# A split attention and feed-forward kernel: the weights' float32 words by an integer add on VectorE, their second parts by one subtraction

## The chip, the cores and the metric

The kernel runs on one core of one Trainium2 chip. The core has TensorE (matmuls, written PE), VectorE (DVE), ScalarE (ACT), GpSimd (POOL) and SyncE (SP, which here only issues transfers). The engines run side by side, each takes its own instructions in the order of the program, and they wait for each other by semaphores. The metric is the device time of one execution in microseconds; the time before is the median of three runs.

## The reference

Block-causal attention over 8 batches of 8 heads, then a feed-forward layer with a maximum over three products:

```python
# q, k, v: 8 x 8 x 576 x 64, float32; w1, w2, w3: 512 x 768, w_out: 768 x 512, float64
scores = scale * np.matmul(q, k.transpose(0, 1, 3, 2))
scores = np.where(block_i >= block_j, scores, -1000000000.0)   # blocks of 64
attn = np.exp(scores - np.max(scores, axis=-1, keepdims=True))
attn = attn / (np.sum(attn, axis=-1, keepdims=True) + 1e-09)
x = np.matmul(attn, v)                                         # as 4608 x 512
h = np.maximum(np.maximum(x @ w1, x @ w2), x @ w3)
return (h @ w_out).astype(np.float32)
```

The weights come as float64, two 32-bit words each. The chip has no float64, so the kernel makes of each weight two parts, a first one `h` rounded to fp32r (the format of TensorE's one-pass matmul) and a second one `l` with what the rounding left.

## The kernel before

**Attention** goes by pairs of heads. A pair loads q and k, transposes them (on VectorE by `turn_qk`, L918; for batch 0 on TensorE, L825), forms the scores (qk, L934 and L941), takes row minima on VectorE (L423), exponentials on ScalarE (L607, L961), scales them on GpSimd or ScalarE (L441, L439), transposes them (L630 and L634; for batch 0 on TensorE, L559 and L987) and multiplies with v (pv, L1001). The result is split into `xh` (ScalarE) and `xl` (GpSimd, L254).

**The feed-forward part** goes by chunks of half a batch (256 or 320 rows). `product` (L1119) forms x times w for six column blocks f and three matrices, each as three fp32r matmuls (wh xh, wh xl, wl xh) over four row blocks. The maximum is taken on VectorE (L1134), split again (`hh`, `hl`), and `project` (L1185) multiplies it with w_out, 128 rows of w_out at a time (`wo` 0 to `wo` 5), three matmuls each.

**The weights** come in 24 units of 128 x 512 numbers: units 0 to 17 are the column blocks of w1, w2 and w3, units 18 to 23 the row blocks of w_out. GpSimd issues the load of a unit (`load`, L293). Then come, before the change:

- `size` (ScalarE, L303): the absolute value of the high words, read as float32;
- `clamp`, `shift`, `sign` (VectorE, L309, L316, L322): limits, a shift by three bits and the sign, which give the float32 `a` that has the float64's upper bits;
- `power` (VectorE, L328): the power of two of `a`; `rest` (VectorE, L339): the low word times that power, `c`, in the tile `left`;
- `high` (ScalarE, L249): `h`, that is `a` rounded to fp32r;
- `whole` (TensorE, L346 to L348): a - h + c in PSUM, by three products with the identity (`plus`) and its negative (`less`); the first is fp32, which runs as two instructions, the others fp32r;
- `lower` (ScalarE, L249): the copy out of PSUM, rounded to fp32r, is `l`.

`a` and one more tile of a unit lie in the place of a w_out tile that isn't loaded yet (`wo0` to `wo5`), for the last two units in output buffers (`osb`). So the loads of w_out wait until such a unit is done.

**The order** of all this is made by a planner (`in_order`): every step is a job with a cost on one engine or a choice of engines, a rank, and slots that it takes and gives; whichever engine is free takes the ready job of the lowest rank. The ranks of a weight unit are `DELAY + PACE * u`. A change of one job's cost or engine moves jobs of all engines.

## Time and profile before

| | us |
|---|---|
| median of three runs | 912.27 |
| lowest, highest run | 911.9, 914.06 |
| span of the profiled execution | 912.0 |
| TensorE busy in it | 892.8 |
| VectorE busy in it | 529.3 |
| ScalarE busy in it | 471.7 |
| GpSimd busy in it | 254.8 |

The profile comes from one execution, whose span, from its first to its last instruction, is 912.0 us. Its page cuts the span into 40 equal slices (22.8 us each) and gives for each the busy share of an engine in tenths (9 is 90% or more) and the clock that TensorE was granted:

```profile
PE   6999899999999999999999999999999999999998
DVE  4999888786545756564555746564554756421111
ACT  3887675666544635545543645546553644522111
PEclk9899999999999999999999999999999999999999
```

The first seven slices, up to 160 us, hold the preparation of the weights, the attention of batch 0 and part of batch 1's, and the first chunk. Behind them TensorE is busy nearly all the time; in the last four there is no attention left.

### The profile page before, as it was taken

What the parts mean: (1) busy time and instruction counts of PE and PEld (TensorE: products, weight loads), DVE (VectorE), ACT (ScalarE), POOL (GpSimd) and SP (SyncE); (2) the same over time, 40 slices, a digit from 0 to 9 for tenths busy, and PEclk for the clock granted to TensorE, in tenths of its full rate; (3) what the DMA queues carried; (4) which work ended last, traced back from release to release, by engine and by line L of the source; (5) the groups of instructions that cost most, each with busy time, mean ns of one, the idle gap of its engine ahead of it and who ended that gap; (6) DMA issues with size and microseconds to landing.
All of it is one profiled execution on the core that took longest, in us unless ns stands there. A gap on an engine that the chain in (4) does not pass through costs nothing.

```text
span 912.0 us, 16897 instructions
## 1 busy us (share of the span) xinstructions
PE 892.8 (98%) x5880; PEld 743.1 (81%) x5880; DVE 529.3 (58%) x1545; ACT 471.7 (52%) x1365; POOL 254.8 (28%) x381
## 2 busy tenths in 40 slices
PE   6999899999999999999999999999999999999998
PEld 4577677777888888888888888888888888899997
DVE  4999888786545756564555746564554756421111
ACT  3887675666544635545543645546553644522111
POOL 3553232243221312223221322233131322222100
PEclk9899999999999999999999999999999999999999
DMA  5772645776554544454554543555553533330010
GB/s 163 202 217 50 135 116 116 167 150 144 106 135 110 104 101 90 115 118 115 112 130 97 105 108 89 125 113 121 112 123 87 118 82 83 97 73 24 1 36 23
DMA packets 226132, 98.36 MB, mean 108 GB/s; under 512 B 189696, under 2 KB 218368, under 8 KB 226048
## 3 DMA queue, kind: packets, MB, share of 16 engines
q1 hardware_dynamic: 208192, 82.35, 40.6%
q0 software_dynamic: 3456, 12.58, 4.4%
q10 hardware_dynamic: 14400, 2.36, 1.4%
q8 instruction: 46, 0.75, 0.3%
q14 instruction: 38, 0.31, 0.1%
HBM read 41.94 MB, written 9.44 MB: 56 GB/s over the span
## 4 chain that ended last, share of the span: by engine, by line
PE 90%; DVE 5%; DMA 1%; ACT 1%; issue 1%; ACTq 0%; POOL 0%; DVEq 0%
PE pm L1119 50%; PE pm L1185 16%; PE sb L1001 10%; PE sb L934 8%; PE sb L941 3%; PE pm L346 1%; DMA nat<-in_q_dram 1%; DVE sb L423 1%; DVE left L339 1%; DVE wo L322 1%; PE sb L559 1%; DMA nat<-in_k_dram 0%; DVE kq L251 0%; ACT p L439 0%; PE pm L348 0%
## 5 line engine op out<-in xcount | busy, mean ns | idle before, releaser
L1119 PE MATMUL pm<-xh,w 128*128 128x320 f32 (+1 forms) x2304 | 498.6, 303 | 0.7 <-ACT xh L249 0.5
L1119 PEld LDWEIGHTS pm<-xh,w 128*128 128x128 f32 x2304 | 378.8, 189 | 18.8 <-issue 14.0
L1119 PE MATMUL pm<-xl,w 128*128 128x256 f32 (+1 forms) x1152 | 340.7, 296 | 0.5 <-DMA nat<-in_k_dram 0.5
L1119 PEld LDWEIGHTS pm<-xl,w 128*128 128x128 f32 x1152 | 218.5, 190 | 6.7 <-issue 5.3
L423 DVE CUSTOM_DVE_ANT_0 sb<-sb,mask 128x512 f32<-128x512 f32 (+3 forms) x288 | 143.7, 530 | 133.5 <-PE sb L941 76.1
L607 ACT ACTIVATE p<-sb,nm 128x256 f32<-128x256 f32 (+3 forms) x256 | 133.9, 527 | 80.2 <-DVE nm L423 73.7
L1134 DVE TENSOR_TENSOR m<-pm,m 128x256 f32<-128x256 f32 (+1 forms) x192 | 85.9, 448 | 147.9 <-PE pm L1119 147.1
L441 POOL TENSOR_TENSOR p<-p,rs 128x128 f32<-128x128 f32 (+4 forms) x133 | 97.9, 755 | 253.9 <-DVE rs L751 194.5
L630 DVE STREAM_TRANSPOSE pz<-p 128x512 f32<-128x512 f32 (+1 forms) x280 | 137.7, 527 | 36.0 <-ACT p L439 19.1
L254 POOL TENSOR_TENSOR hl<-m,hh 128x256 fp32r<-128x256 f32 x96 | 71.5, 745 | 248.4 <-ACT hh L249 216.5
L1185 PE MATMUL pm<-wo,hh 128*128 128x512 f32 x384 | 119.2, 392 | 0.0
L439 ACT ACTIVATE p<-p,rs 128x512 f32<-128x512 f32 (+4 forms) x155 | 88.2, 597 | 20.6 <-DVE rs L751 14.1
L249 ACT CAST hh<-m 128x256 fp32r<-128x256 f32 x96 | 38.8, 405 | 110.1 <-DVE m L1134 109.1
L934 PE MATMUL sb<-kq 64*128 64x256 f32 (+3 forms) x512 | 89.1, 466 | 3.2 <-DVE kq L251 3.1
L1001 PE MATMUL sb<-pt,vn 128*64 128x320 f32 (+4 forms) x840 | 90.2, 363 | 0.4 <-DVE pt L251 0.3
L254 POOL TENSOR_TENSOR xl<-x,xh 128x256 fp32r<-128x256 f32 (+1 forms) x64 | 52.7, 829 | 130.9 <-ACT xh L249 130.9
L1001 PEld LDWEIGHTS sb<-pt,vn 128*64 128x64 f32 x840 | 55.1, 137 | 34.5 <-issue 1.7
L1185 PEld LDWEIGHTS pm<-wo,hh 128*128 128x128 f32 x384 | 70.9, 188 | 14.9 <-issue 0.3
L934 PEld LDWEIGHTS sb<-kq 64*128 64x128 f32 x512 | 46.3, 192 | 38.1 <-issue 20.8
L1185 PE MATMUL pm<-wo,hl 128*128 128x512 f32 x192 | 74.9, 390 | 0.0
L249 ACT COPY osb<-pm 128x512 f32<-128x512 f32 x36 | 21.1, 587 | 69.5 <-PE pm L1185 67.4
L249 ACT COPY m<-pm 128x256 f32<-128x256 f32 (+1 forms) x96 | 38.1, 397 | 32.6 <-PE pm L1119 23.9
(82 smaller groups left out, 764.0 us busy)
## 6 DMA issues: line engine op xcount, KB each, us to landing
pt<-pz SPq DMA_DIRECT2D x224, 200.0 KB, 3.9
w<-in_moe_w_dram POOLq DMA_DIRECT2D x18, 512.0 KB, 5.2
vn<-in_v_dram SPq DMA_DIRECT2D x64, 128.0 KB, 2.4
out_dram<-osb SPq DMA_DIRECT2D x32, 256.0 KB, 2.0
nat<-in_k_dram SPq DMA_DIRECT2D x112, 72.0 KB, 2.4
nat<-in_q_dram SPq DMA_DIRECT2D x96, 72.0 KB, 2.5
wo<-in_moe_w_out_dram POOLq DMA_DIRECT2D x6, 512.0 KB, 4.4
nat<-in_q_dram ACTq DMA_DIRECT2D x16, 72.0 KB, 4.3
```

What stands on the lines that cost most here:

```text
L249: nc.scalar.copy(dst, src)
L254: {"DVE": nc.vector, "POOL": nc.gpsimd}[eng].tensor_tensor(out=dst, in0=a, in1=b, op=ALU.subtract)
L423: nc.vector.tensor_tensor_reduce(out=ps, in0=ps, in1=hidden, scale=-SCALE, scalar=first, op0=ALU.add, op1=ALU.min, accum_out=out_)
L439: nc.scalar.mul(p, p, r)
L441: nc.gpsimd.tensor_tensor(out=p, in0=p, in1=r.broadcast_to([P, p.shape[1]]), op=ALU.mult)
L607: nc.scalar.activation(dst, src, AF.Exp, bias=nm[:, c : c + 1], scale=-1.0, accum_out=sm[:, c : c + 1])
L630: nc.vector.transpose(dst, p[:, 0 : n * P])
L934: nc.tensor.matmul(ps, self.q[h.own, P * t : P * (t + 1)], self.k[h.own, 0:w], start=True, stop=True)
L1001: nc.tensor.matmul(o[h.own].rearrange("p (i u) -> p i u", u=n)[:, :, c0 : c0 + z - a], self.vn[:, kt, h.j, :], h.pt[:, :, h.off + a : h.of ...
L1119: nc.tensor.matmul(self.ps, w[i, f][:, c, :], xx, start=(c == 0 and s == 0), stop=(c == NC - 1 and s == 2))
L1134: nc.vector.tensor_tensor(out=m, in0=ps, in1=m, op=ALU.max)
L1185: nc.tensor.matmul(self.po[: self.rows], h, w[f], start=(f == 0 and s == 0), stop=(f == NF - 1 and s == 2))
```

## The change

The float32 word is now made whole before it is split. A new step `tail` takes the low word times 2^-29 as an integer (the bits that `shift` left out, rounded), on ScalarE or VectorE as the planner chooses; `whole` is one integer add of these bits to `a`, on VectorE; `high` rounds the sum to `h` as before; `lower` is one subtraction a - h, on GpSimd or VectorE. `power` and `rest`, the three products with the identity, the copy out of PSUM, the tile `less` and the use of `left` by the weights are gone. The temporary tiles are now given back by `lower`.

```diff
-    less = const.tile([P, P], F32R, name="less")
-    nc.scalar.mul(less, one, -1.0)
...
-            for step, fast in (
-                (self.clamp, True),
-                (self.shift, True),
-                (self.sign, False),
-                (self.power, True),
-                (self.rest, False),
-            ):
+            k = job({"ACT": act(512, False) + 65.0, "DVE": dve(512) + 80.0}, rank, self.tail, after=(j,))
+            for step, fast in ((self.clamp, True), (self.shift, True), (self.sign, False), (self.whole, False)):
                 c = dve(512, fast) + (130.0 if fast else 80.0)
-                e = "DVE"
-                j = job({e: c}, rank, step, after=(j,), take=("left",) if step == self.rest else (), lasts=c + GAP)
-            j = job({"ACT": act(512, False)}, rank, self.high, after=(j,))
-            j = job({"PE": 6 * pe(512)}, rank, self.whole, after=(j,), take=("pm",), give=(*self.temps, "left"))
-            self.done = job({"ACT": act(512)}, rank, self.lower, after=(j,), give=("pm",))
+                j = job({"DVE": c}, rank, step, after=(j, k) if step == self.whole else (j,), lasts=c + GAP)
+            h = job({"ACT": act(512, False)}, rank, self.high, after=(j,))
+            self.done = job({"POOL": pool(512), "DVE": dve(512) + 80.0}, rank, self.lower, after=(h,), give=self.temps)
...
+        def tail(self, eng):
+            b = self.parts()[1].bitcast(I32)
+            if eng == "ACT":
+                nc.scalar.mul(b, self.low_word, 2.0**-29)
+            else:
+                nc.vector.tensor_scalar(out=b, in0=self.low_word, scalar1=2.0**-29, scalar2=None, op0=ALU.mult)
...
         def whole(self, eng):
-            self.ps = psm.tile([P, 512], F32, name="pm")
-            nc.tensor.matmul(self.ps, plus.bitcast(F32), self.a, start=True, stop=False)
-            nc.tensor.matmul(self.ps, less, self.h, start=False, stop=False)
-            nc.tensor.matmul(self.ps, plus, self.c, start=False, stop=True)
+            a = self.a.bitcast(I32)
+            nc.vector.tensor_tensor(out=a, in0=a, in1=self.b.bitcast(I32), op=ALU.add)
...
         def lower(self, eng):
-            copy(eng, self.l, self.ps)
+            minus(eng, self.l, self.a, self.h.bitcast(F32))
```

The planner gives 19 of the 24 `tail` steps to ScalarE and 5 to VectorE, and 14 of the 24 `lower` steps to GpSimd and 10 to VectorE. In the changed kernel line numbers differ: L423 becomes L408, L1119 becomes L1104, L1185 becomes L1170, L1001 becomes L986, L934 becomes L919, L309, L316 and L322 become L312, L319 and L325; the integer add is L333. A number behind a name tells copies of a tile apart.

TensorE, before, at the end of the first stretch: the last unit's products and the first projection that needs `wo` 5 (`wo_1799`).

```order
L934 MATMUL sb<-kq 128x256 x2
L346 MATMUL pm<-osb,plus 128x512
L347 MATMUL pm<-wo_1799,less 128x512
L348 MATMUL pm<-left,plus 128x512
L1001 MATMUL sb<-pt,vn_75 64x320 x6
L1001 MATMUL sb<-pt,vn_75 64x4x48 x2
L1001 MATMUL sb<-pt,vn_75 64x4x16 x2
L1185 MATMUL pm<-wo_1799,hh_1616 128x512 x2
```

Now, ahead of the projection that needs `wo` 5 (`wo_1627`):

```order
L1104 MATMUL pm<-xh_1333,w_656 128x320
L1104 MATMUL pm<-xl_1350,w_656 128x320
L1104 MATMUL pm<-xh_1333,w_656 128x320
L1104 MATMUL pm<-xh_1474,w_656 128x320
L1104 MATMUL pm<-xl_1483,w_656 128x320
L1104 MATMUL pm<-xh_1474,w_656 128x320
L1170 MATMUL pm<-wo_1627,hh_1319 128x512 x2
```

The three products with the identity are gone, the pv group that stood between them and the projection has moved behind it, and products stand there; between the projections that need `wo` 4 and `wo` 5 are 36 of them and one qk group (two L919 of 512, 384 and 128 columns each).

VectorE, before, the steps of the last unit (its tiles are `osb` and `wo_1598`) among the attention's reductions:

```order
L309 TENSOR_SCALAR osb<-osb 128x512
L423 ISA sb,nm<-sb,mask 128x128
L423 ISA nm 128x1
L316 TENSOR_SCALAR osb<-osb 128x512
L423 ISA sb,nm<-sb,mask 128x384
L423 ISA nm 128x1
L322 SCALAR_TENSOR_TENSOR osb<-wo_1598,osb 128x512
L423 ISA sb,nm_1769<-sb,mask 128x512
L423 ISA nm_1769 128x1
L328 TENSOR_SCALAR osb<-osb 128x512
L423 ISA sb,nm_1769<-sb,mask,nm_1769 128x64
L423 ISA nm_1769 128x1
```

Now, from the subtraction of the unit before it (`wo_1530`) to the last integer add:

```order
L252 TENSOR_TENSOR wo_1530<-osb,wo_1530 128x512
L1119 TENSOR_TENSOR m<-pm,m 128x320
L957 SCALAR_TENSOR_TENSOR rs_1487<-sm_1486 128x1
L903 STREAM_TRANSPOSE kq<-nat 128x1152
L312 TENSOR_SCALAR osb<-osb 128x512
L963 RECIPROCAL rs_1487<-rs_1487 128x1
L319 TENSOR_SCALAR osb<-osb 128x512
L732 TENSOR_SCALAR rs<-sm 128x2
L325 SCALAR_TENSOR_TENSOR osb<-wo_1441,osb 128x512
L736 RECIPROCAL rs<-rs 128x2
L333 ISA osb<-osb 128x1024
```

The reductions that stood between the last unit's steps stand elsewhere, and the unit ends with the add, which the order prints with 1024 columns.

GpSimd, now, at the loads of w_out (before, no subtraction of weights stood there):

```order
L252 TENSOR_TENSOR w_1183<-wo_941,w_1183 128x512
L284 DMA wo_1209<-in_moe_w_out_dram 128x1024
L252 TENSOR_TENSOR w_1215<-wo_966,w_1215 128x512
L284 DMA wo_1249<-in_moe_w_out_dram 128x1024
L252 TENSOR_TENSOR wo_1285<-wo_1198,wo_1285 128x512
```

The loads now follow subtractions on the same engine.

More of the change, by code (lines that the diff above doesn't have):

```diff
@@ L295, in load, with parts @@
             self.low_word, self.high_word = lo_hi[:, :, 0].bitcast(U32), lo_hi[:, :, 1]
-        def size(self, eng):
-            if len(self.temps) == 1:
-                w = moe.tile([P, 2, 512], F32, name=self.temps[0], bufs=1)
-                self.a, self.b = w[:, 0], w[:, 1]
-            else:
-                self.a, self.b = (moe.tile([P, 512], F32, name="osb", bufs=slots["osb"]) for _ in range(2))
-            nc.scalar.activation(self.a, self.high_word.bitcast(F32), AF.Abs)
+        def parts(self):
+            if not hasattr(self, "a"):
+                if len(self.temps) == 1:
+                    w = moe.tile([P, 2, 512], F32, name=self.temps[0], bufs=1)
+                    self.a, self.b = w[:, 0], w[:, 1]
+                else:
+                    self.a, self.b = (moe.tile([P, 512], F32, name="osb", bufs=slots["osb"]) for _ in range(2))
+            return self.a, self.b
+        def tail(self, eng):
+            b = self.parts()[1].bitcast(I32)
+            if eng == "ACT":
+                nc.scalar.mul(b, self.low_word, 2.0**-29)
+            else:
+                nc.vector.tensor_scalar(out=b, in0=self.low_word, scalar1=2.0**-29, scalar2=None, op0=ALU.mult)
+        def size(self, eng):
+            nc.scalar.activation(self.parts()[0], self.high_word.bitcast(F32), AF.Abs)
         def clamp(self, eng):
@@ L324, in sign @@
             )
-        def power(self, eng):
-            nc.vector.tensor_scalar(
-                out=self.b.bitcast(I32),
-                in0=self.a.bitcast(I32),
-                scalar1=-(2**23),
-                scalar2=None,
-                op0=ALU.bitwise_and,
-            )
-        def rest(self, eng):
-            parts = moe.tile([P, 2, NF, P], F32R, name="left", bufs=1)
-            self.c = parts[:, 0, 0:4].rearrange("p f q -> p (f q)")
-            nc.vector.scalar_tensor_tensor(
-                out=self.c, in0=self.low_word, scalar=2.0**-52, in1=self.b, op0=ALU.mult, op1=ALU.mult
-            )
         def whole(self, eng):
-            self.ps = psm.tile([P, 512], F32, name="pm")
-            nc.tensor.matmul(self.ps, plus.bitcast(F32), self.a, start=True, stop=False)
-            nc.tensor.matmul(self.ps, less, self.h, start=False, stop=False)
-            nc.tensor.matmul(self.ps, plus, self.c, start=False, stop=True)
+            a = self.a.bitcast(I32)
+            nc.vector.tensor_tensor(out=a, in0=a, in1=self.b.bitcast(I32), op=ALU.add)
         def high(self, eng):
```

## The prediction

> **What bounds the kernel now.** I read the engines' shares first, then the busy times by stretch, then the chain of work that ended last. The first line is the page's list of engines (busy us, share of the span, instructions). The next three are stretches that I chose: start:end, length, busy us and instructions of PE, PEld, DVE, ACT and POOL, granted clock, DMA share and rate.
>
> ```profile
> PE 892.8 (98%) x5880; PEld 743.1 (81%) x5880; DVE 529.3 (58%) x1545; ACT 471.7 (52%) x1365; POOL 254.8 (28%) x381
> 0.00:20.00 20.00, 12.03 (x50) 8.26 (x50) 8.01 (x36) 6.78 (x22) 6.82 (x19) 1.00 0.61 170
> 20.00:148.10 128.10, 121.55 (x702) 87.08 (x702) 114.99 (x293) 95.74 (x255) 48.21 (x61) 0.97 0.57 145
> 153.30:912.00 758.70, 754.08 (x5099) 644.77 (x5097) 401.59 (x1202) 365.62 (x1075) 198.10 (x300) 1.00 0.45 101
> ```
>
> From 153.3 us on TensorE lacks 4.6 us of being always busy, and VectorE is at 53%: that stage is worth what TensorE has to do in it. From 20 to 148.1 us it is different: TensorE is busy 121.6 of 128.1 us, but VectorE 115.0 of them, with 13.1 us idle. Both engines are nearly full there, and all weight products that the change drops lie in this stretch, but for unit 23's just behind it. So the question is which of the two ends it afterwards.
>
> Where the stretch ends is in the timeline and in the chain (start us, length us, what):
>
> ```profile
> 147.39 0.69 DVE L339 SCALAR_TENSOR_TENSOR left<-wo,osb 128x512 fp32r<-128x512 uint32 x1
> 149.58 1.05 PE pm L346 x2
> 150.64 0.23 PE pm L347
> 150.87 0.24 PE pm L348
> 151.10 2.21 PE sb L1001 x20
> 151.59 0.59 ACT L249 CAST wo<-pm 128x512 fp32r<-128x512 f32 x1
> 153.31 5.00 PE pm L1185 x21
> ```
>
> VectorE's last weight step ends at 148.1 us, the products of unit 23 at 151.1, its second part at 152.2; at 153.3 TensorE takes the first projection that needs `wo` 5. I call this the anchor, since it stands in both orders with nearly the same work behind it, and TensorE cannot pass it before all weights are there.
>
> **What goes from TensorE.** One unit, in the timeline:
>
> ```profile
> 72.91 1.02 PE L346 MATMUL pm<-wo,plus 128*128 128x512 f32 x2
> 73.37 0.79 PE L347 MATMUL pm<-w,less 128*128 128x512 f32 x1
> 74.00 0.39 PE L348 MATMUL pm<-left,plus 128*128 128x512 f32 x1
> 74.23 0.98 PE L987 MATMUL sb<-plus,p 128*128 128x128 f32 x5
> ```
>
> From 72.91 to 74.23 is 1.32 us of TensorE for a unit (the listed lengths overlap), 24 units 31.7 us. Were TensorE the only bound, this would be the gain. It isn't: behind it stands VectorE's queue.
>
> **What VectorE has to do up to the anchor.** Groups with line, form, count, then busy us and mean ns of one:
>
> ```profile
> L328 DVE TENSOR_SCALAR wo<-wo 128x512 int32<-128x512 int32 x22 | 10.7, 489 | 0.0
> L328 DVE TENSOR_SCALAR osb<-osb 128x512 int32<-128x512 int32 x2 | 0.8, 400 | 0.0
> L339 DVE SCALAR_TENSOR_TENSOR left<-w,wo 128x512 fp32r<-128x512 uint32 x18 | 13.0, 724 | 1.3 <-PE pm L348 1.3
> L339 DVE SCALAR_TENSOR_TENSOR left<-wo,wo 128x512 fp32r<-128x512 uint32 x4 | 3.4, 852 | 0.1
> L339 DVE SCALAR_TENSOR_TENSOR left<-wo,osb 128x512 fp32r<-128x512 uint32 x2 | 1.3, 664 | 0.0
> L322 DVE SCALAR_TENSOR_TENSOR wo<-w,wo 128x512 int32<-128x512 int32 x18 | 12.9, 723 | 0.1
> L918 DVE STREAM_TRANSPOSE kq<-nat 128x1152 f32<-128x1152 f32 x28 | 38.1, 1361 | 3.4 <-DMA nat<-in_q_dram 3.1 <-PE sb L934 0.2
> ```
>
> Removed are `power` (L328) and `rest` (L339): 10.7 + 0.8 + 13.0 + 3.4 + 1.3 = 29.2 us, and L339's wait of 1.3 us for TensorE. Added are 24 integer adds, which the trace does not show. The nearest row is L322: two sources of 512 words, 0.72 us. The order prints the add as 128x1024, and L918 takes 1361 ns for 1152 columns, 1.21 us for 1024: that is the upper end; the one-source L328, 0.49, is the lower. I take 0.72, because the words are 512: 24 x 0.72 = 17.4 us. Ten of the 24 subtractions stand on VectorE, two sources again: 7.2 us. Five `tail` steps stand there, between L328 and L322, say 0.6: 3.0 us. Added in all 27.6, so the edit itself takes only 1.6 us off VectorE.
>
> What else moved is counted in the two orders, up to the last `rest` before and the last add now: 100 rows of L423 for 114, so 7 reductions with their 7 accumulator reads fewer; no L630 or L634 transposes for 12; 38 copies of L251 for 35.
>
> ```profile
> L423 DVE CUSTOM_DVE_ANT_0 sb<-sb,mask 128x512 f32<-128x512 f32 (+3 forms) x288 | 143.7, 530 | 133.5 <-PE sb L941 76.1 <-PE sb L934 45.9 <-ACT p L607 6.7
> L630 DVE STREAM_TRANSPOSE pz<-p 128x512 f32<-128x512 f32 (+1 forms) x280 | 137.7, 527 | 36.0 <-ACT p L439 19.1 <-POOL p L441 14.7
> L251 DVE COPY pt<-sb 128x256 f32<-128x256 f32 (+3 forms) x12 | 4.7, 400 | 0.1
> ```
>
> 7 x 0.53 + 12 x 0.53 - 3 x 0.40 = 8.8 us moved behind the anchor. VectorE's work from 20 us on becomes 115.0 - 29.2 + 27.6 - 8.8 = 104.6 us, 10.4 less.
>
> **ScalarE and GpSimd.** 24 copies out of PSUM go from ScalarE, 19 `tail` steps come; 14 subtractions come on GpSimd.
>
> ```profile
> L249 ACT CAST w<-pm 128x512 fp32r<-128x512 f32 x18 | 10.5, 585 | 4.8 <-PE pm L348 2.1 <-PE sb L559 1.5 <-PE pm L1119 1.2
> L303 ACT ACTIVATE wo<-w 128x512 f32<-128x512 f32 x18 | 12.4, 699 | 1.4 <-issue 1.1 <-ACT wo L303 0.4
> L441 POOL TENSOR_TENSOR p<-p,rs 128x512 f32<-128x512 f32 x27 | 29.2, 1087 | 4.6 <-PE sb L1001 4.3 <-DVE rs L751 0.4
> 66.05 3.28 POOL L441 TENSOR_TENSOR p<-p,rs 128x384 f32<-128x384 f32 x3 [1.44 <-DVE rs L751]
> 66.53 1.90 DVE L309 TENSOR_SCALAR wo<-wo 128x512 f32<-128x512 f32 x2
> L309 DVE TENSOR_SCALAR wo<-wo x22: 396/426/1366, 19.5 to 122.1; 128x512 f32<-128x512 f32 x22
> L309 DVE TENSOR_SCALAR wo<-wo 128x512 f32<-128x512 f32 x22 | 12.5, 579 | 1.6 <-ACT wo L303 1.6
> ```
>
> ScalarE: 24 x 0.59 = 14.0 off, 19 x 0.70 = 13.3 on, no change. GpSimd: 14 x 1.09 = 15.2 us on, in a stretch where it was busy 48.2 of 128.1 us, 38%. That has a price on VectorE: two clamps (L309) took 1.90 us while GpSimd's tensor operations ran; the line's durations are 396 at least and 579 ns on average, 0.18 lost per instruction. 48 of this kind stay (L309 and L316), 8.8 us lost at 38%; at (48.2 + 15.2) / 119.9 = 53% it would be 3.5 us more.
>
> VectorE's last add then ends at 148.1 - 10.4 - 1.3 + 3.5 = 139.9 us, with the rest of its idle time left as it is: waits for TensorE may shrink, but waits for ScalarE's `tail` and `high` come instead.
>
> **From there to the anchor.** `wo` 5 still needs the cast (0.59, as the copy above), the subtraction on GpSimd (1.09) and three hand-overs, 0.4 us in all by my estimate (the one above, from TensorE to ScalarE, took at most 151.59 - 151.11 = 0.48): 139.9 + 0.59 + 1.09 + 0.4 = 142.0 us. Beside it runs TensorE's own queue: `wo` 4 has its subtraction on VectorE ten rows before the last add: L918 1.36, two at 0.72, clamp and shift at 0.58, one max step and four short ones, an estimated 1.3 together, so 5.3 us. Its projection starts at 139.9 - 5.3 + 0.2 = 134.8; then one qk group, 36 products and the projection itself stand before the anchor.
>
> ```profile
> 117.43 1.93 PE sb L934 x12
> 127.38 1.04 PE sb L941 x4
> 832.65 31.99 PE pm L1119 x222
> 205.60 8.38 PE pm L1185 x36
> ```
>
> 1.93 + 36 x 0.144 + 3 x 0.233 = 7.8 us: 142.6. The later of the two, **142.6**, is the anchor now, 10.7 us earlier.
>
> Behind it TensorE's order has 12 products of 320 columns fewer (-1.7), one pv group more (+2.2, L1001 above), one L941 pair (+1.0) and two of L934's twelve (+0.6, by columns): 2.1 us more. So the span becomes 912.0 - 10.7 + 2.1 = 903.4, and 0.3 lies around it (the median of the runs is 912.27, the profiled span 912.0): **903.7 us**, 0.9% faster. TensorE's 31.7 us go, and some 21 come back as its idle time ahead of the anchor.
>
> **Rivals.**
>
> *TensorE sets the pace throughout*: the whole 31.7 us, 880.6. Against it: VectorE would have to do its 104.6 us between 20 us and about 117. Chance 0.03.
>
> *VectorE closes its gaps.* With TensorE no longer full, the 13.1 us idle and the 3.5 for GpSimd may go; all of it gives 888, half 896. For it: some of the gaps are waits for TensorE. Chance 0.14, 888 to 896.
>
> *The integer add is dear* (the other side). Each 0.1 us on it is 2.4 us on VectorE's queue ahead of the anchor, with nothing to cover it. From 0.72 + 8.6 / 24 = 1.08 us on nothing is gained; at L918's rate, 1.21, the time is 915.5. Against it: the words are 512. Chance 0.10. The Trainium skill, "VectorE: DVE Perf Modes", section "The perf-mode tier table", gives two-source operations two 16-bit elements a cycle but one of fp32; were the 1024 elements run one a cycle, an estimate by that page's formula is (1024 + 151) / 0.96 GHz = 1.22 us, and no run here shows it yet.
>
> *TensorE's clock falls.* Three stretches of 5 us: busy us and instructions of PE, granted clock, DMA share, GB/s.
>
> ```profile
> 20.00:25.00 5.00, 3.04 (x18) 0.94 0.66 148
> 25.00:30.00 5.00, 4.69 (x15) 0.50 0.64 211
> 30.00:35.00 5.00, 5.00 (x29) 0.88 0.86 265
> ```
>
> After 5 us with TensorE 61% busy the clock was 0.50 for 5 us, which costs 2.5 us and 0.9 in the two beside it. Ahead of the anchor TensorE would now be busy 12.0 + 121.6 + 5.2 (148.1 to 153.3, all busy) - 31.7 - 2.1 = 105.0 of 142.6 us, 74%, so this may come back several times. TensorE has some 21 us of slack there, so most is hidden; where a reduction on VectorE waits for qk, one to four such falls could give 905 to 917. Chance 0.12. The Trainium skill, "TensorE: Matmul & The Clock Gate", section "What's actually happening", has the array at half clock after an idle window of about 3.4 us and at full clock after as long a busy one; the half clock at 25 us agrees with it, and by that rule short gaps such as these would cost nothing.
>
> *The last weights arrive late*, since GpSimd issues their loads behind a subtraction that waits for ScalarE: 905 to 914, chance 0.06. That the products stay is excluded by TensorE's order.
>
> **Chances and range.** The forecast itself, 896 to 910, has 0.55. Below 896 lie 0.17; the dear add, the clock and the loads hold 0.28. A measurement tells 0.3%, 2.7 us, from no change: faster 0.52 + 0.17 + 0.05 + 0.04 = 0.78, the same 0.03 + 0.03 + 0.03 + 0.01 = 0.10, slower 0.12. The range, 890 to 914, takes in half-closed gaps and most of the dear add, and leaves out about 0.2.
>
> **What would show it.** Right: no L346 to L348; the integer add at 0.6 to 0.8 us; VectorE still about 88% busy from 20 us to its last add, near 140 us; TensorE some 30 us idle before that and at most 5 after; the projection that needs `wo` 5 near 143 us. Wrong: adds over 1 us, a last add before 132 or after 146 us, clamps well above 0.64 us, or more idle time of TensorE behind the anchor than before, which would mean that the attention work moved behind it costs there.

## The result, and the profile after

| | us |
|---|---|
| median of four runs after | 919.72 (918.77 to 922.85) |
| median of four runs before, beside them | 912.16 (911.9 to 914.06) |
| ratio | 1.0074, 95% interval 1.0049 to 1.0098 |
| span of the profiled execution after | 921.1 |

The change makes the kernel 0.7% slower; forecast were 903.7 us and 0.9% faster. The profiled execution is the run of 922.85 us, 3.1 us above the median, so the sums below are of this one execution.

From the page of the changed kernel, its list of engines and the slices (23.0 us each now) of two of them and of the clock:

```profile
PE 878.3 (95%) x5784; PEld 736.1 (80%) x5784; DVE 539.1 (59%) x1538; ACT 469.5 (51%) x1354; POOL 278.8 (30%) x398
...
PE   6787789999999999999999999999999999999998
...
DVE  4999989876664656464664656464664655421111
...
PEclk9979889999999999999999999999999999999999
```

In the first six slices TensorE has gaps now and a lower clock, and VectorE is as full as before. Three stretches of the same kernel (start:end, length, busy us and instructions of PE, PEld, DVE, ACT and POOL, granted clock, DMA share, GB/s):

```profile
0.00:20.00 20.00, 12.24 (x51) 8.42 (x52) 8.01 (x36) 7.21 (x23) 6.97 (x19) 1.00 0.60 170
20.00:150.37 130.37, 103.58 (x608) 76.82 (x608) 118.41 (x261) 90.25 (x232) 70.11 (x76) 0.88 0.49 129
152.42:921.10 768.68, 760.43 (x5115) 648.77 (x5113) 410.68 (x1238) 371.38 (x1099) 199.65 (x302) 1.00 0.45 102
```

TensorE has lost 14.5 us of busy time in all, but stands idle for 42.8 us (921.1 - 878.3) where it was 19.2. From 20 us to the end of the last integer add VectorE has 118.4 us to do in 130.4; before it had 115.0 in 128.1. So the queue that sets the end of this stretch has not become shorter, although 32 instructions fewer were recorded in it (293 before). TensorE's clock is 0.88 there, and was 0.97. From the timelines of TensorE and VectorE of the changed kernel, the places that the prediction named:

```profile
144.21 0.75 PE L1170 MATMUL pm<-wo,hh 128*128 128x512 f32 x2
149.65 0.69 DVE L333 CUSTOM_DVE_ANT_0 osb<-osb 128x1024 uint16<-128x1024 uint16 x1
152.42 0.77 PE L1170 MATMUL pm<-wo,hh 128*128 128x512 f32 x2
```

These are the projection of `wo` 4, the last add and the projection of `wo` 5, which is the anchor: 152.4 us, where 142.6 had been forecast and 153.2 stood before. Behind it 768.7 us follow; 758.8 stood before and 760.8 were forecast. The miss of 17.7 us in the span is 9.8 us at the anchor and 7.9 behind it.

What fills VectorE shows in its groups between 20 us and its last weight step. First three of the kernel before (the sign, the clamp and the old steps stand in the prediction), then the changed kernel's; count, then busy us and mean ns of one.

```profile
L316 DVE TENSOR_SCALAR wo<-wo 128x512 int32<-128x512 int32 x22 | 11.8, 547 | 0.1
L972 DVE SCALAR_TENSOR_TENSOR rs<-sm 128x1 f32<-128x1 f32 x5 | 1.3, 255 | 0.0
L747 DVE TENSOR_SCALAR rs<-sm 128x4 f32<-128x4 f32 x6 | 1.0, 170 | 0.2 <-ACT p L607 0.2
```

```profile
L333 DVE CUSTOM_DVE_ANT_0 wo<-wo 128x1024 uint16<-128x1024 uint16 x22 | 17.7, 806 | 0.0
L325 DVE SCALAR_TENSOR_TENSOR wo<-w,wo 128x512 int32<-128x512 int32 x18 | 14.6, 809 | 0.1
L325 DVE SCALAR_TENSOR_TENSOR wo<-wo,wo 128x512 int32<-128x512 int32 x4 | 3.9, 967 | 0.0
L319 DVE TENSOR_SCALAR wo<-wo 128x512 int32<-128x512 int32 x22 | 14.3, 652 | 0.0
L312 DVE TENSOR_SCALAR wo<-wo 128x512 f32<-128x512 f32 x21 | 12.1, 581 | 0.0
L732 DVE TENSOR_SCALAR rs<-sm 128x4 f32<-128x4 f32 x6 | 3.7, 615 | 0.0
L957 DVE SCALAR_TENSOR_TENSOR rs<-sm 128x1 f32<-128x1 f32 x5 | 2.9, 581 | 0.0
```

The view of the add's line adds its shortest, median and longest duration in ns, and its first and last start:

```profile
L333 DVE CUSTOM_DVE_ANT_0 wo<-wo x22: 643/682/1430, 23.1 to 130.6; 128x1024 uint16<-128x1024 uint16 x22
```

The same instructions take longer than before: the sign (L322, now L325) from 0.72 and 0.69 us for its two large groups to 0.81 and 0.97, the shift from 0.55 to 0.65, and a sum of four elements in a row (L747, now L732) from 0.17 to 0.62. The add has a median of 0.68 us and single ones of up to 1.43. A sum of so few elements does not take longer because of its data; something stops it. The timeline of VectorE and GpSimd shows what:

```profile
98.41 0.68 DVE L325 SCALAR_TENSOR_TENSOR wo<-w,wo 128x512 int32<-128x512 int32 x1
98.43 1.79 POOL L252 TENSOR_TENSOR w<-wo,w 128x512 fp32r<-128x512 f32 x1
99.01 0.41 DVE L1119 TENSOR_TENSOR m<-pm,m 128x256 f32<-128x256 f32 x1
99.42 1.36 DVE L333 CUSTOM_DVE_ANT_0 wo<-wo 128x1024 uint16<-128x1024 uint16 x1
...
147.74 1.25 POOL L426 TENSOR_TENSOR p<-p,rs 128x576 f32<-128x576 f32 x1 [0.50 <-DVE rs L963]
147.91 1.11 DVE L732 TENSOR_SCALAR rs<-sm 128x2 f32<-128x2 f32 x1
```

At 147.91 us VectorE takes a sum of two elements; it ends at 149.02, just after GpSimd's multiplication (148.99). At 99.42 an add starts under GpSimd's subtraction (until 100.22) and takes 1.36 us, twice its time. The sign at 98.41 started just ahead of that subtraction and took its usual 0.68; and the maximum at 99.01, which reads PSUM, ran through in 0.41 beside it.

Taken together are VectorE's instructions from 15 to 160 us that read and write SBUF: the weights' steps and the sums, but no reductions, copies and maxima out of PSUM, no transposes and reciprocals, no multiplications of p. "Beside" are those that share over 0.1 us with an instruction of GpSimd that computes (no issues of transfers); "lost" is what these took beyond the shortest of their form in all the kernels of this document.

| kernel | taken | beside | lost, us | lost by the others, us |
|---|---|---|---|---|
| before | 137 | 41 | 13.8 | 3.8 |
| after | 125 | 64 | 24.8 | 2.7 |

So the kernel before lost by this already, and the change adds 11.0 us. Transposes and reciprocals also work in SBUF, but did not lose: in the changed kernel a transpose of 512 columns took 0.69 us beside GpSimd and 0.68 without.

That is theory A, contention: GpSimd's subtractions lengthen VectorE's instructions, and VectorE's queue sets the anchor. The rival B is the clock: gaps on TensorE lower it, its late results hold VectorE. Theory D is for the stage behind the anchor alone: attention's work, put behind the weights by the order, comes late there.

### The profile page after: what moved, and what is told of

Its sections match the earlier page's. It is cut to its first block, busy times and chain, and to the rows that moved or that the text cites. A ratio compares the mean times of both kernels' runs of the same rounds, so it can differ in the third digit from the quotient of the medians.

```text
span 921.1 us, 16695 instructions
## 1 busy us (share of the span) xinstructions
PE 878.3 (95%) x5784; PEld 736.1 (80%) x5784; DVE 539.1 (59%) x1538; ACT 469.5 (51%) x1354; POOL 278.8 (30%) x398
## 4 chain that ended last, share of the span: by engine, by line
PE 82%; DVE 11%; DMA 2%; ACT 2%; issue 1%; SPq 1%; POOL 1%; ACTq 0%; DVEq 0%; POOLq 0%
PE pm L1104 45%; PE pm L1170 15%; PE sb L986 10%; PE sb L919 8%; PE sb L926 3%; DVE sb L408 2%; DMA pt<-pz 1%; DVE wo L325 1%; DVE pz L615 1%; DVE wo L333 1%; DVE wo L319 1%; SPq L627 1%; PE sb L544 1%; DVE wo L312 1%; DVE m L1119 1%
## 5 line engine op out<-in xcount | busy, mean ns | idle before, releaser
L1104 PE MATMUL pm<-xh,w 128*128 128x320 f32 (+1 forms) x2304 | 503.4, 305 | 3.9 <-POOL w L252 2.1
L1104 PEld LDWEIGHTS pm<-xh,w 128*128 128x128 f32 x2304 | 382.6, 191 | 22.5 <-issue 14.4
L1104 PE MATMUL pm<-xl,w 128*128 128x256 f32 (+1 forms) x1152 | 343.1, 298 | 1.1 <-POOL xl L252 1.1
L1104 PEld LDWEIGHTS pm<-xl,w 128*128 128x128 f32 x1152 | 220.8, 192 | 7.0 <-issue 4.8
L408 DVE CUSTOM_DVE_ANT_0 sb<-sb,mask 128x512 f32<-128x512 f32 (+3 forms) x288 | 143.4, 529 | 132.5 <-PE sb L926 78.3
L592 ACT ACTIVATE p<-sb,nm 128x128 f32<-128x128 f32 (+3 forms) x256 | 133.8, 527 | 86.5 <-DVE nm L408 81.5
L426 POOL TENSOR_TENSOR p<-p,rs 128x128 f32<-128x128 f32 (+4 forms) x136 | 102.6, 773 | 236.4 <-DVE rs L736 195.0
L1119 DVE TENSOR_TENSOR m<-pm,m 128x256 f32<-128x256 f32 (+1 forms) x192 | 85.8, 447 | 143.2 <-PE pm L1104 142.4
L1170 PE MATMUL pm<-wo,hh 128*128 128x512 f32 x384 | 120.2, 394 | 1.7 <-POOL wo L252 1.1
L986 PE MATMUL sb<-pt,vn 128*64 128x320 f32 (+4 forms) x840 | 94.1, 367 | 4.6 <-DMA pt<-pz 2.4
L919 PE MATMUL sb<-kq 64*128 64x256 f32 (+3 forms) x512 | 91.0, 474 | 4.1 <-DVE kq L249 3.1
L247 ACT CAST hh<-m 128x256 fp32r<-128x256 f32 x96 | 38.9, 405 | 108.3 <-DVE m L1119 105.7
L986 PEld LDWEIGHTS sb<-pt,vn 128*64 128x64 f32 x840 | 57.0, 139 | 40.4 <-issue 8.3
L1170 PEld LDWEIGHTS pm<-wo,hh 128*128 128x128 f32 x384 | 71.0, 188 | 16.9 <-POOL wo L252 1.6
L919 PEld LDWEIGHTS sb<-kq 64*128 64x128 f32 x512 | 47.3, 196 | 40.3 <-issue 22.9
L1170 PE MATMUL pm<-wo,hl 128*128 128x512 f32 x192 | 75.1, 391 | 0.0
```

Of the source, the lines that this page charges most:

```text
L247: nc.scalar.copy(dst, src)
L408: nc.vector.tensor_tensor_reduce(out=ps, in0=ps, in1=hidden, scale=-SCALE, scalar=first, op0=ALU.add, op1=ALU.min, accum_out=out_)
L426: nc.gpsimd.tensor_tensor(out=p, in0=p, in1=r.broadcast_to([P, p.shape[1]]), op=ALU.mult)
L592: nc.scalar.activation(dst, src, AF.Exp, bias=nm[:, c : c + 1], scale=-1.0, accum_out=sm[:, c : c + 1])
L919: nc.tensor.matmul(ps, self.q[h.own, P * t : P * (t + 1)], self.k[h.own, 0:w], start=True, stop=True)
L986: nc.tensor.matmul(o[h.own].rearrange("p (i u) -> p i u", u=n)[:, :, c0 : c0 + z - a], self.vn[:, kt, h.j, :], h.pt[:, :, h.off + a : h.of ...
```

## The experiments

Each was run beside the kernel before on the same chip; ratios are to that, with their 95% interval. Its median there was 913.3 to 914.2 us. "Lost" is the sum above.

### Same order, one part smaller: e1, e2, e3, g2

**e1**, GpSimd's subtractions on an eighth of the columns:

```diff
-            minus(eng, self.l, self.a, self.h.bitcast(F32))
+            n = 64 if eng == "POOL" else 512
+            if eng == "POOL":
+                (wol if self.last else wl)[self.dst] = (woh if self.last else wh)[self.dst]
+            minus(eng, self.l[:, :n], self.a[:, :n], self.h.bitcast(F32)[:, :n])
```

> The changed kernel with GpSimd's 14 subtractions cut to 64 of their 512 columns, every instruction in its place; the third product of those 14 units reads the first parts again, so the second parts of these units are left out of the result. Contention (theory A: GpSimd's subtractions lengthen VectorE's SBUF-to-SBUF instructions, and VectorE's queue sets the anchor): mean of the integer add (L333) from 0.80 to 0.70 us or less, of the shift (L319) from 0.64 to 0.56 or less, of the four-element sums (L732) from 0.6 to 0.3 or less; VectorE's busy time from 20 us to its last add from 118 to about 110 us; last add from 149.7 to 140-144 us; time 909 to 914 us. Clock (theory B: gaps on TensorE lower its clock ahead of the anchor, and VectorE waits for late products): busy time may shrink, but its waits grow in its place, last add within 2 us of 149.7, time 917 to 921.

Measured: 911.68 us (0.9974, 0.9959 to 0.9990). Its stretch up to the end of the last add, then two of its groups:

```profile
20.00:141.08 121.08, 97.68 (x607) 73.98 (x608) 110.87 (x261) 89.17 (x232) 57.98 (x76) 0.92 0.52 139
```

```profile
L333 DVE CUSTOM_DVE_ANT_0 wo<-wo 128x1024 uint16<-128x1024 uint16 x22 | 16.3, 739 | 0.0
L319 DVE TENSOR_SCALAR wo<-wo 128x512 int32<-128x512 int32 x22 | 11.1, 504 | 0.0
```

VectorE executes the same 261 instructions in 110.9 us, 7.5 less, and the last add starts at 140.4 us, 9.3 earlier. Lost: 18.1 (58 beside). The time, the last add and the shift fall as A had it; the add (0.74, forecast 0.70 at most) and the sums of four (0.46, forecast 0.3) do not fall as far; GpSimd's other work, the normalisations of attention, still lies beside them (f1 to f4 take that up). It is GpSimd's work that lengthens VectorE's, and VectorE's queue moves the anchor (143.2 us now).

**e2**, the integer add on an eighth of its words:

```diff
-            nc.vector.tensor_tensor(out=a, in0=a, in1=self.b.bitcast(I32), op=ALU.add)
+            n = 64
+            nc.vector.tensor_tensor(out=a[:, :n], in0=a[:, :n], in1=self.b.bitcast(I32)[:, :n], op=ALU.add)
```

> The changed kernel with each integer add on 64 of its 512 words, every instruction in its place; the low words' bits of the other 448 columns are left out of the weights. It takes some 24 x 0.6 = 14 us from VectorE's queue ahead of the anchor. If VectorE's queue sets the anchor (A): last add from 149.7 to 136-141 us, wo 5's projection from 152.4 to 141-145 (TensorE's own queue then holds it), time 907 to 913. If TensorE's low clock and the waits for it do (B): VectorE's idle time before the last add grows from 12 us to over 20, last add at 145 or later, time 915 to 920.

Measured: 907.62 us (0.9943, 0.9921 to 0.9966). The stretch up to the end of the last add, then that add and the anchor in the timeline:

```profile
20.00:137.65 117.65, 93.32 (x602) 69.16 (x601) 107.84 (x261) 88.39 (x232) 67.39 (x76) 0.97 0.53 141
```

```profile
137.41 0.22 DVE L334 CUSTOM_DVE_ANT_0 osb<-osb 128x128 uint16<-128x128 uint16 x1
140.18 0.63 PE L1171 MATMUL pm<-wo,hh 128*128 128x512 f32 x2
```

VectorE is idle for 9.8 us there. Lost: 26.1, about as in the changed kernel. 10.6 us off VectorE's queue bring the last add and the anchor 12.2 us forward: the queue sets the anchor about one for one, as the prediction had it.

**e3**, TensorE filled again where it idles, by four identity products of which nothing is used:

```diff
             if c == 0:
                 self.ps = psm.tile([P, self.n], F32, name="pm")
+                if self.first:
+                    for _ in range(4):
+                        nc.tensor.matmul(self.ps, plus.bitcast(F32), mask[:, : self.n], start=True, stop=True)
```

> The changed kernel with four identity products of 256 columns (results overwritten) ahead of the first product of each of the 18 groups of the first chunk, some 30 us of TensorE's work back in the place where it idled; nothing else moves. Clock (B): the granted clock from 60 to 150 us rises from 0.86 to 0.95 or more, TensorE's work no longer stretches, last add at 143 us or earlier, time 912 or less. Contention (A): the clock may rise, but VectorE's instructions stay as long (L333 mean 0.78 to 0.83), last add within 2 us of 149.7 or later, time 917 to 923.

Measured: 932.66 us (1.0198, 1.0175 to 1.0221), outside both expectations. The clock is 0.96 up to the anchor (0.90 in the changed kernel), the last add comes at 162.7 us, 13 us later, the anchor at 165.5; lost: 24.0. VectorE is busy 118.7 us as before, but its idle time has grown from 12.0 to 24.7 us, with waits for TensorE. B's forecast is missed, but the run does not settle it: the added products do not fit into the gaps, and what a better clock gave could be hidden under what they cost.

**g2**, the same with `range(1)`:

> The changed kernel with one identity product of 256 columns (result overwritten), not four, ahead of the first product of each of the 18 groups of the first chunk: some 7.5 us of TensorE's work. If the clock has a share in the late anchor (B): clock from 20 us to the last add above 0.91 (0.88 without the products), last add at 148 us or earlier, time 918 or less. If it has none (A): last add 150 to 155, wo 5's projection 152.4 to 157, time 919 to 925.

Measured: 917.57 us (1.0044, 1.0027 to 1.0061). The stretch up to the end of the last add, then that add in the timeline:

```profile
20.00:150.36 130.36, 104.87 (x641) 78.56 (x642) 118.95 (x261) 89.97 (x232) 69.80 (x76) 0.93 0.49 128
```

```profile
149.67 0.69 DVE L333 CUSTOM_DVE_ANT_0 osb<-osb 128x1024 uint16<-128x1024 uint16 x1
```

The clock went from 0.88 to 0.93, and the last add stands within 0.02 us where it stood. So the low clock that g2 lifted, ahead of 120 us (60 to 80 us: 1.00 for 0.76; 100 to 120: 0.91 for 0.83), has no share in the late last add. From 130 us to the anchor the clock is 0.86 in both kernels, so g2 does not test it there. The time lies in B's range (918 or less) and 1.4 us below A's; by the profile that difference lies behind the anchor (763.7 us there, 768.7 in the changed kernel), and the last add and the anchor (152.7 us) are A's.

### Another engine for the second parts: e4, e5, e6, e7

Here the planner orders anew. **e4**, the second parts by TensorE:

```diff
+    less = const.tile([P, P], F32R, name="less")
+    nc.scalar.mul(less, one, -1.0)
...
-            self.done = job({"POOL": pool(512), "DVE": dve(512) + 80.0}, rank, self.lower, after=(h,), give=self.temps)
+            j = job({"PE": 5 * pe(512)}, rank, self.differ, after=(h,), take=("pm",), give=self.temps)
+            self.done = job({"ACT": act(512)}, rank, self.lower, after=(j,), give=("pm",))
...
-            minus(eng, self.l, self.a, self.h.bitcast(F32))
+            copy(eng, self.l, self.ps)
+        def differ(self, eng):
+            self.ps = psm.tile([P, 512], F32, name="pm")
+            nc.tensor.matmul(self.ps, plus.bitcast(F32), self.a, start=True, stop=False)
+            nc.tensor.matmul(self.ps, less, self.h, start=False, stop=True)
```

> The integer add kept, but the second parts by two identity products on TensorE (a float32 one of the sum, one of the first part) and ScalarE's copy out of PSUM: no subtraction on GpSimd or VectorE; the planner orders anew. TensorE gets about 24 x 1.1 = 26 us back. Contention (A): L333 at 0.70 us or less, shift at 0.56 or less, VectorE's busy time from 20 us to its last add 102 to 107 us, last add at 138 to 143, wo 5's projection at 141 to 147, time 903 to 910, below both kernels. Clock alone (B) would give a clock of 0.95 or more ahead of the anchor and a gain too, but with VectorE's instructions as long as in the changed kernel. If neither: 915 or more.

Measured: 914.44 us (1.0007, 0.9994 to 1.0021), as the kernel before; forecast were 903 to 910. VectorE's queue did become short (100.3 us, last add at 134.1, lost 11.8, shift 0.48 us), but the add stayed at 0.80 us, and the anchor, 139.6 us, can't be compared: 771.1 us follow it, among them 37 product matmuls more than in the changed kernel (3207, 3170 there). TensorE was full again ahead of it (106.4 of 114.8 us). An anchor is a measure only between kernels of one order.

**e5**, all subtractions on VectorE:

```diff
-            self.done = job({"POOL": pool(512), "DVE": dve(512) + 80.0}, rank, self.lower, after=(h,), give=self.temps)
+            self.done = job({"DVE": dve(512) + 80.0}, rank, self.lower, after=(h,), give=self.temps)
```

> All 24 subtractions on VectorE (14 more there, 14 x 0.72 = 10 us), none on GpSimd; the planner orders anew. Contention (A): the lengthening that the one-eighth subtractions took back (7.5 us of VectorE's busy time) and some more of it goes, the 10 us come: VectorE's busy time from 20 us to its last add 118 to 122, last add 148 to 153 us, shift at 0.52 us or less, time 916 to 922, about the changed kernel's. If only the amount of work on VectorE counts and not who works beside it: last add at 158 us or later, time 926 or more.

Measured: 918.77 us (1.0056, 1.0036 to 1.0075). Fourteen subtractions more on VectorE did not lengthen the kernel: lost fell from 24.8 to 15.5 (43 beside), which about pays the 10 us. The shift was not the one that gained (0.65 us, forecast 0.52), the sums and the adds were (0.17 and 0.69 us): which instructions GpSimd meets depends on the order. VectorE was busy 110.5 us (forecast 118 to 122) and the last add, at 141.1, was 7 us earlier than forecast, but over 771 us followed the anchor.

**e6** and **e7**, the even units by TensorE as in e4, the odd ones by VectorE alone (e6, whose edit this is) or by GpSimd or VectorE (e7):

```diff
+            self.by_pe = u % 2 == 0
+            if self.by_pe:
+                j = job({"PE": 5 * pe(512)}, rank, self.differ, after=(h,), take=("pm",), give=self.temps)
+                self.done = job({"ACT": act(512)}, rank, self.lower, after=(j,), give=("pm",))
+            else:
+                self.done = job({"DVE": dve(512) + 80.0}, rank, self.lower, after=(h,), give=self.temps)
...
```

> Second parts of the 12 even units by two identity products on TensorE and ScalarE's copy, of the 12 odd ones by subtraction on VectorE, none on GpSimd. Contention (A): VectorE has 2 subtractions more than in the changed kernel and loses at least 7.5 us of lengthening, TensorE gets 12 x 1.1 = 13 us of its idle 30 back: last add 139 to 144, time 906 to 912, below both kernels. If TensorE's work ahead of the anchor costs as in the run with the filling products (30 us gave 13 us later), 13 us cost 6 and the time is 912 to 917.

> Second parts of the 12 even units by TensorE and ScalarE, of the odd ones by GpSimd or VectorE as the planner has it. About half of GpSimd's subtractions and of VectorE's go. Contention (A): half of the lengthening of 7.5 us and 3 to 4 us of subtractions off VectorE, last add 141 to 146, time 908 to 914; L319 between 0.50 and 0.62 us. Without contention it would lie with the run that has none on GpSimd within 2 us.

Measured: e6 915.19 us (1.0024, 1.0004 to 1.0043), e7 917.25 us (1.0042, 1.0028 to 1.0056). Both miss the gain; e6 lies in the range given for TensorE's work costing as in e3, and e7, 2.1 us above e6, at the edge of what was to speak against contention. Lost: 17.0 and 18.2. No split of this one step that was run beats the kernel before.

### The stage behind the anchor: e8

```diff
-    PACE = 3.5
+    PACE = 4.0
```

> The changed kernel with the weights' ranks stretched from 3.5 to 4.0 a unit: attention's work goes ahead of late weights in the order. If the time behind the anchor (765 to 769 us in four kernels with the changed order, 758.8 before) comes from attention work put behind the weights (theory D), it falls to 763 or less and the anchor comes later, 153 to 160 us; time 914 to 921. If it does not come from the order, it stays at 765 or more and the time rises to 920 or more.

Measured: 916.33 us (1.0035, 1.0015 to 1.0055); anchor at 154.6 us, 765.1 us behind it. The stage became 3.6 us shorter, but not below 765: by its own numbers the run leaves D open. Its profile, too, is of its longest run, 921.46 us, so those two numbers say little of the median.

### GpSimd's other work: f1, f2, f3, f4

If A is right, the normalisations on GpSimd lengthen VectorE's steps too. They go, for batches 0 and 1, to VectorE or ScalarE:

```diff
-    def norm_cost(n):
+    def norm_cost(n, early=False):
+        if early:
+            return {"DVE": dve(n, True) + 130.0, "ACT": 190.0 + n / 1.2}
...
+        elif eng == "DVE":
+            nc.vector.tensor_scalar(out=p, in0=p, scalar1=r, scalar2=None, op0=ALU.mult)
...
-                self.scales[t] = job(norm_cost(P * (t + 1)), r, self.scale, t, after=(self.inv[t],))
+                self.scales[t] = job(norm_cost(P * (t + 1), not part.beside), r, self.scale, t, after=(self.inv[t],))
...
-            self.scaled = job(norm_cost(S), first + 7, self.scale4, after=(inv,), give=("stat4",))
+            self.scaled = job(norm_cost(S, not self.part.beside), first + 7, self.scale4, after=(inv,), give=("stat4",))
```

f1 is this on the changed kernel, f2 on e5, f3 on the kernel before, f4 on e4.

> The changed kernel with the normalisations of batches 0 and 1 taken off GpSimd, to VectorE or ScalarE by the planner's choice (39 short multiplications on VectorE, an estimated 39 x 0.35 = 14 us); GpSimd keeps 20 subtractions of weights, VectorE 4. Contention (A): VectorE's SBUF-to-SBUF instructions lose less than the 23 us of the changed kernel, about as long as only the subtractions lie beside them (10 to 14 us), six subtractions (4 us) go from VectorE: its gain of 13 to 17 us about pays the 14 us; time 911 to 918. If GpSimd's normalisations cost VectorE nothing, only the 14 - 4 = 10 us come: 925 or more.

> All 24 subtractions on VectorE and the normalisations of batches 0 and 1 on VectorE or ScalarE: GpSimd has only the second parts of x and of the hidden layer left ahead of the anchor. Contention (A): VectorE's SBUF-to-SBUF instructions beside GpSimd lose 5 us or less in all (23 in the changed kernel, 14 with the subtractions alone moved); the integer add, shift and sign at 0.70, 0.45 and 0.72 us or less on average; time 912 to 919. If they stay longer than this, something other than GpSimd lengthens them.

> The kernel before with the normalisations of batches 0 and 1 on VectorE (36 of them, about 12 us) or ScalarE. Contention (A): VectorE loses 3 us or less in place of 9, so it has about 6 us more to do in all; 914 to 920.

> Integer add, second parts by two identity products on TensorE and a copy on ScalarE, and the normalisations of batches 0 and 1 on VectorE (44, about 15 us) or ScalarE. Contention (A): VectorE loses 3 us or less beside GpSimd; 912 to 918, no better than the same kernel with the normalisations on GpSimd (914.4). Below 911 it would beat both kernels.

| run | us | ratio | beside | lost, us |
|---|---|---|---|---|
| f1 | 916.35 | 1.0025 (1.0005 to 1.0045) | 40 | 15.2 |
| f2 | 916.19 | 1.0028 (1.0011 to 1.0046) | 26 | 6.1 |
| f3 | 913.28 | 0.9997 (0.9987 to 1.0008) | 17 | 3.6 |
| f4 | 911.68 | 0.9980 (0.9967 to 0.9993) | 19 | 3.5 |

What is lost follows what GpSimd is given: 24.8 with both, 15.2 with the subtractions, 15.5 with the normalisations (e5), 6.1 with neither; of the kernel before, without subtractions, 13.8 with the normalisations and 3.6 without. In f2 the shift takes 0.42 us and the sign 0.71 on average; the add, at 0.80, stays above the 0.70 forecast, for single adds still meet what is left to GpSimd. The times of f1 and f2 came as forecast: what is no longer lost pays what VectorE is given. f3 and f4 came a little better than forecast, and f4 0.2% below the kernel before.

### A version below both: g3, and what it needs: h1 to h4

g3 is f4 with `PACE = 4.0`; h1 is f3 with it (no integer add), h2 the kernel before with it, h3 is e4 with it (normalisations on GpSimd), h4 is f4 with 4.5.

> The kernel with the second parts by TensorE and the normalisations of batches 0 and 1 off GpSimd (911.7), with the weights' ranks stretched from 3.5 to 4.0 a unit. With GpSimd out of the way VectorE's queue is short of TensorE's, so placing weights later should neither open nor close much: 909 to 914 by A. If late weights hold TensorE, 915 or more.

> The kernel before with the normalisations of batches 0 and 1 off GpSimd and the weights' ranks at 4.0 a unit; no integer add. If the combined kernel's gain needs the integer add (its TensorE has 24 x 0.24 us and its VectorE 24 x 0.5 us less to do), this one stays at 910 to 915; if the placing of the weights gives it, it comes to 908 or less.

> The kernel before with the weights' ranks at 4.0 a unit and nothing else. TensorE and VectorE are both full ahead of the anchor whatever the order: 911 to 917. At 908 or less the rank alone gives the gain.

> Integer add, second parts by two identity products on TensorE, ranks at 4.0 a unit, normalisations left on GpSimd. If GpSimd's work beside VectorE's is what still holds it (A), it lies above the combined kernel's 905.6 by 3 to 8 us: 908 to 914. If not, within 2 us of it.

> The combined kernel with the ranks at 4.5 a unit. If later weights keep feeding TensorE from attention first: 903 to 906; if the weights then come too late for the first products: 907 to 912.

| run | us | ratio |
|---|---|---|
| g3 | 905.60 | 0.9909 (0.9891 to 0.9926) |
| h1, no integer add | 911.47 | 0.9971 (0.9959 to 0.9983) |
| h2, the rank alone | 914.53 | 1.0009 (0.9996 to 1.0021) |
| h3, normalisations on GpSimd | 911.17 | 0.9973 (0.9957 to 0.9988) |
| h4, rank 4.5 | 907.52 | 0.9918 (0.9885 to 0.9950) |

g3 was forecast at 909 to 914; it is 8 us below the kernel before. h1, h2 and h3 came as their own theories had it, h4 at the lower end of the second of its two, weights that come too late. The stretch of g3 up to the end of its last add, then three of its groups:

```profile
20.00:140.50 120.50, 115.95 (x694) 82.22 (x691) 111.52 (x312) 98.25 (x253) 30.10 (x38) 1.00 0.55 145
```

```profile
L336 DVE CUSTOM_DVE_ANT_0 wo<-wo 128x1024 uint16<-128x1024 uint16 x22 | 15.7, 716 | 0.0
L328 DVE SCALAR_TENSOR_TENSOR wo<-w,wo 128x512 int32<-128x512 int32 x18 | 12.3, 682 | 0.0
L322 DVE TENSOR_SCALAR wo<-wo 128x512 int32<-128x512 int32 x22 | 9.5, 432 | 0.0
```

GpSimd has 30.1 us to do there, for 70.1 in the changed kernel; the sign and the shift are at 0.68 and 0.43 us; lost 3.2. TensorE's clock is 1.00. The integer add, the normalisations off GpSimd and the rank are each needed: without the add it is 911.5 (h1), with the normalisations on GpSimd 911.2 (h3), at the old rank 911.7 (f4), and the rank alone gives nothing (h2). Whether the second parts must be TensorE's was not tried at this rank (at 3.5, f1 and f2 have 916.4 and 916.2). Why the rank gives 6 us here, which was not forecast, is open: in the profiles the anchor of g3 is 10 us later than that of f4 (145.8, 135.4) and the stage behind it 13 us shorter (758.4, 771.6), as D would have it, but no run isolates it.

## Why the prediction was wrong, point by point

**TensorE's 31.7 us** went as forecast: the products are gone, and TensorE idles 34.6 us ahead of the anchor (152.42 less 117.87 busy; "some 30" were named). Its busy time fell by 14.5 us only: up to the anchor what is left took 117.9 us where 105.0 were forecast, most of it stretched by the lower clock (e2, at a clock of 0.98 up to its anchor, has 108.3), and behind it there was more to do.

**The integer add** at 0.72 us is right as a price: median 0.68. The rival of a dear add, 1.08 us or more, falls, and with it the 1.22 us that the prediction worked out from the Trainium skill, "VectorE: DVE Perf Modes", for 1024 elements. In all the adds took 19.1 us, not 17.4, because single ones were stopped.

**VectorE's work** was to be 104.6 us plus "3.5 us more" for GpSimd. This 3.5, the price of GpSimd's added work on VectorE, is the step that failed. Measured are 118.4. The moved work is right: by the groups 5.4 us of reductions and 5.1 of transposes fewer and 1.8 of copies more, 8.7 for the 8.8 forecast. Against the prices used, the sign took 3.0 us more, the shift 2.1, the sums of one to six elements 5.3, the adds 1.7, the ten subtractions 1.0, the tails 0.7 less, the clamp 0.1 less: 12.3 us where 3.5 were allowed; 1.5 us more are spread over the rest. The prediction saw the contention in two clamps, took a mean loss of 0.18 us on 48 clamps and shifts, and scaled it with GpSimd's busy share, 38 to 53%. On these 48 it was not far off: those beside GpSimd lost 8.3 us before and 9.9 now, and the clamps, whose growth was to be its sign, stayed at 0.59 us on average. What it left out are the other steps, which are stopped as well, down to the two-element sums: signs and sums lost 2.2 us before and 9.9 now, the new adds and subtractions 4.8, where `power` and `rest` had lost 3.2. In all 64 of 125 steps lie beside GpSimd for 41 of 137, and the loss of one grew from 0.34 to 0.39 us (13.8 / 41, 24.8 / 64). GpSimd's own instructions also grew: the group below, forecast at 1.09 us, took 1.38.

```profile
L252 POOL TENSOR_TENSOR w<-wo,w 128x512 fp32r<-128x512 f32 x11 | 15.2, 1382 | 24.3 <-ACT w L247 24.2
```

The rule stands in the Trainium skill, "SBUF — State Buffer", section "Who interferes with whom": VectorE's instructions with two inputs in SBUF, or in a mode that takes both of its ports, share one pair of SBUF ports with GpSimd, whichever starts first holds it for its whole instruction, and the other does not run slower but stops. The rows above agree: the two-element sum that ended 0.03 us behind GpSimd's multiplication, and the sign that started 0.02 us ahead of a subtraction and lost nothing. By that rule the loss goes with the number of meetings, not with a share; it bears on this change and was not weighed.

**VectorE's idle time** is right: 12.0 us, forecast 11.8. So its last add ended at 150.4 and not at 139.9 us, all of it by busy time; e1 and e2 show that the queue moves the anchor.

**The anchor by TensorE's own queue** is right in its form: it lies 8.2 us behind the projection of `wo` 4 (7.8 forecast), which is late by 9.4 us (144.2, forecast 134.8). But TensorE came to `wo` 4 in its own queue too. Its last waits ahead of the anchor are at `wo` 2, for ScalarE's cast and GpSimd's subtraction of that unit, whose add ended on VectorE at 127.4 us; the first two rows show the subtraction and the projection behind it. From there TensorE works without a wait for 22.6 us, at a low clock (third row). `wo` 5 was ready only just in time, by GpSimd's subtraction in the last row:

```profile
128.32 1.48 POOL L252 TENSOR_TENSOR wo<-wo,wo 128x512 fp32r<-128x512 f32 x1 [1.68 <-ACT wo L247]
129.85 0.80 PE L1170 MATMUL pm<-wo,hh 128*128 128x512 f32 x1 [1.06 <-POOL wo L252]
129.85:152.42 22.57, 22.57 (x123) 16.30 (x124) 19.57 (x49) 12.12 (x35) 9.68 (x12) 0.86 0.64 126
151.34 1.29 POOL L252 TENSOR_TENSOR wo<-osb,wo 128x512 fp32r<-128x512 f32 x1
```

So the prediction's two ways, 142.0 and 142.6 us, meet within 0.3 us again, at 152.6 and 152.4. Both hang on VectorE's queue. In e2 the same stretch of TensorE took 20.3 us at a clock of 1.00; but a full clock here would have met a `wo` 5 that is not done before 152.6 us.

**The clock** fell, as the rival said: 0.76 from 60 to 80 us, 0.83 from 100 to 140, and lowest in the stretch below; the row behind it, from the view of waits (total, times, longest), has TensorE's longest wait between 5 us and the anchor.

```profile
60.00:65.00 5.00, 3.96 (x19) 3.67 (x19) 4.97 (x11) 3.69 (x10) 2.23 (x4) 0.50 0.79 261
```

```profile
PE sb L972 <- ACT p L592: 5.2, 3, 3.0
```

So the clock fell with no longer gap than 3.0 us in TensorE's work, where the prediction let short gaps cost nothing. The half clock at 25 us in the kernel before, too, follows no single long gap, as the prediction read it: from 21.0 to 24.4 us TensorE was busy 1.7 us, its longest wait between 5 and 31 us was 1.4 us, and its one wait of 4.8 us, at the start, was followed by a clock of 1.00 up to 20 us. But the clock was not what held the last add (g2).

**Behind the anchor** 2.1 us more were forecast and 9.9 measured: the second term that was too small, and its cause is only in part shown. Four runs of the same order as the changed kernel (e1, e2, e3, g2) have 763.7 to 767.9 us there: about 5 to 9 above the kernel before whatever happened ahead of it. In e2, whose clock there is full, TensorE has 4.4 us more to do (758.5 busy, 754.1 before), not 2.1: the pv group was priced from a row of 20 instructions, at 2.2 us, and pv grew by 4.3 (80.9 to 85.2 us). The rest of the changed kernel's 9.9 is 3.6 us more idle time (8.2, before 4.6) and 1.9 of stretched work (760.4 less e2's 758.5). TensorE's timeline shows both, for two pv groups before and two after:

```profile
169.85 3.72 PE L1001 MATMUL sb<-pt,vn 128*64 128x320 f32 x28
185.88 2.93 PE L1001 MATMUL sb<-pt,vn 128*64 128x320 f32 x28
```

```profile
164.47 2.89 PE L986 MATMUL sb<-pt,vn 128*64 128x320 f32 x26 [1.30 <-DMA pt<-pz]
197.45 4.58 PE L986 MATMUL sb<-pt,vn 128*64 128x320 f32 x26 [1.82 <-issue]
```

A pv group now waits 1.3 us for its transposes, which were moved behind the last add. Another starts after 1.8 us of idle time for which the profile names no cause, and takes 4.6 us for 26 products where the first took 2.9; the clock was 0.51 from 197.5 to 200.9 us. The prediction put nothing on such waits, and named more idle time of TensorE behind the anchor as a sign of being wrong. That the transposes come late because the order puts them behind the weights (D) is argued from the order and these waits; e8 did not settle it, and no run took these transposes forward.

**The time around the span**, 0.3 us, was another small error: in the later runs it is 1.8 us for both kernels (922.85 less 921.1). So the span of 912.0 and the median of 912.27 were hardly of one execution.

## What to carry to other kernels

Before moving work to GpSimd or to an SBUF-to-SBUF step of VectorE, count in the timeline how often the two meet and what each meeting costs; the price of an instruction is its undisturbed duration plus its meetings, and a two-element sum can cost a microsecond. Where one queue is nearly full, taking 32 us off the other is worth only what the full one loses too. When an order changes, price what moved behind a mark by whole groups with their waits, and compare marks only between kernels of one order.

## What the runs showed of the hardware that was not expected

An exact 32-bit integer add of 512 words on VectorE, listed as 1024 16-bit elements, takes 0.68 us, as long as other steps with two sources of 512 words (0.68 us where undisturbed, L325). VectorE's reductions out of PSUM did not lose beside GpSimd: 0.70 us for 512 columns beside it and 0.69 without, in the changed kernel. In the changed kernel the granted clock fell to 0.50 although the longest recorded wait of TensorE between 5 us and the anchor was 3.0 us.
